# The last stage of an output sum, in four quarters of 144 columns on four row groups of one bank

## The chip, the cores and the metric

The kernel runs on one core of a Trainium2 chip. Its time is the device time of one launch in microseconds; lower is better. Three runs of the kernel before gave 210.95, 211.09 and 211.11 us. The inputs are fixed.

Five engines work on a core, each with its own instruction queue in order: TensorE (PE, with its weight loads shown apart as PEld), VectorE (DVE), ScalarE (ACT), GpSimd (POOL) and SyncE (SP). POOL, SP and ACT also issue DMA transfers between the chip's memory (HBM) and the on-chip memory (SBUF). Matmul results go to PSUM, which has eight banks; a bank holds 512 float32 values on each of 128 partitions.

## The reference

One decoding step for 4 sequences: a sliding-window attention over cached keys and values, and a small mixer MLP, both on the same normalised row of 576 values, added to the input.

```python
xn = layernorm(x)                      # x: 4 x 1 x 576
q  = (xn @ wq)                         # 32 heads of 128
k, v = k_cache[:, :, -2048:], v_cache[:, :, -2048:]     # 16 key/value heads, each for 2 query heads
a  = softmax(q k^T / sqrt(128)) v @ wo
h  = gelu(layernorm(xn) @ w1); hs = shifted(h) @ w2     # B_w1, B_w2
x1 = xn + hs
return x + a + x1 + gelu(layernorm(x1) @ w3) @ w4       # w3: 576 x 4608, w4: 4608 x 576
```

`shifted` moves each quarter of h by one or two places along a sequence of length 1 and fills with zeros, so hs is zero and x1 is xn. The kernel therefore loads neither w1 nor w2, before and after the change: it adds x and xn, and normalises xn again for the MLP. It loads the keys and values of the window, wq, wo, w3 and w4, 87.2 MB in all.

## The kernel before

The order of the work is written out by hand; each engine runs its instructions in the order in which the code names them, and the framework adds semaphores where one engine reads or overwrites what another wrote.

**Start.** SP issues wq (4.6 MB in two transfers) and ACT issues x at once. POOL builds index tiles, two identity matrices and small constants (`neg_half`, `zero`), then the tile `fold` (L234). ACT clears tiles that need zeros, through the helper `cleared` (L211): `xnT`, `ln2T`, `qz`. The layernorm of x alternates between DVE and POOL (the power -0.5 is on POOL, L268), and its result is transposed on PE (L282, L284) with the help of a tile `dup` that POOL fills (L277, L279). POOL then copies selection matrices (L303, L319, L329), and only after those does `start_loads` issue the first two loads of keys (L125, an indirect DMA of 4.2 MB each). A second layernorm, the first part of wo and the first load of values follow on POOL.

**Main part.** Eight steps, each over two of the 16 key/value heads: keys are transposed on DVE (L297), scores computed on PE (L411), softmax spread over DVE, ACT and PE, and values multiplied on PE (L475). Three buffers hold keys and values; a buffer that is freed lets POOL issue the next load, so that several loads always wait in POOL's DMA queue. w3 comes between the values, wo in four parts, and w4 last, in six pieces of 18, 7, 5, 4, 1 and 1 of its 36 blocks (`W4_PIECES`). The MLP's first matrix and its activation are done in step 3; the activation's result is the tile `gT`, 36 blocks of 4 columns, written by POOL (L569).

**The output sum.** Everything that is added to the output is a product of 128x4 weights with 128x576 data, cut in two halves of 288 columns. `acc` is one PSUM bank in which four groups of 4 rows (at rows 0, 32, 64, 96) take such halves in turn: group 0 and 2 the first half, 1 and 3 the second (L230). At the end the four groups must be added in pairs. That is done by copying `acc` to SBUF (`half`, L244) and a float32 matmul with `fold`, a 0/1 matrix of 128 x 4 for each half (L257), into two further PSUM banks, `sum0` (rows 0 to 3) and `sum1` (rows 32 to 35). The last eleven blocks of w4 go straight to those two banks (L252): five ahead of the fold, so that ACT's copy stands beside them, and six behind it. DVE copies the first half of the result to the SBUF tile `fin` (L719), ACT the second (L721), and SP stores 4 rows of 576 bfloat16 values (L722).

Of the kernel before, what the change touches and what calls it, by code (L numbers as in the profile page):

```python
# [8 lines left out]
ACT = mybir.ActivationFunctionType  # L9
ALU = mybir.AluOpType  # L10
AX = mybir.AxisListType
BF16 = mybir.dt.bfloat16
F32 = mybir.dt.float32
# [9 lines left out]
def kernel(  # L23
# [14 lines left out]
    nc = tc.nc  # L38
    P = 128
    B, Sq, D = A_x.shape  # L40
# [8 lines left out]
    NF = F // P  # L49
# [3 lines left out]
    QD = 32  # L53
# [5 lines left out]
    QC = 2 * SC  # L59
    NI = 2  # L60
    CW = D // NI
    NW = SC * QD
    assert NW == 512 and NSL * NJ == QD and NQ == 2 * NQD * NW and NFH == 18
    scale = float(Dh) ** -0.5
# [5 lines left out]
    o2 = out.flatten_outer_dims()  # L70
# [12 lines left out]
    const = ctx.enter_context(tc.tile_pool(name="const", bufs=1))  # L83
    small = ctx.enter_context(tc.tile_pool(name="small", bufs=2))
    ps_s = ctx.enter_context(tc.tile_pool(name="ps_s", bufs=3, space=PSUM))
# [43 lines left out]
    first = wop.tile([P, WOR * D], BF16, tag="wo", name="first")  # L129
# [26 lines left out]
    W4_PIECES = [0, NFH, NF - 11, NF - 6, NF - 2, NF - 1, NF]  # L156
# [50 lines left out]
    def cleared(shape, name):  # L207
        t = const.tile(shape, BF16, name=name)
        flat = t[:] if len(shape) == 2 else t[:].rearrange("p a b -> p (a b)")
        flat = flat.bitcast(F32)  # L210
        nc.scalar.activation(out=flat, in_=zero[:].bitcast(F32).to_broadcast(list(flat.shape)), func=ACT.Copy)  # L211
        return t
# [2 lines left out]
    ln2T = cleared([P, KJ + 2, QD], "ln2T")  # L215
    ZP = (NSL - 1) * NJ
    qz = cleared([P, ZP + NPR * 4 * P], "qz")
    gT = const.tile([P, NF, B], BF16, name="gT")
    op = const.tile([P, WOR, B], BF16, name="op")

    acc = ps_acc.tile([P, CW], F32, name="acc")
    nc.vector.memset(acc[:], 0.0)

    def acc_of(g):
        return acc[g * QD:g * QD + B, :]

    def acc_matmuls(terms):
        for k, (lhsT, rhs) in enumerate(terms):
            for i in range(NI):
                nc.tensor.matmul(out=acc_of(k % 2 * NI + i), lhsT=lhsT, rhs=rhs[:, i * CW:(i + 1) * CW],  # L230
                                 start=False, stop=False, skip_group_check=True)

    fold = const.tile([P, NI * B], F32, name="fold")
    nc.gpsimd.tensor_tensor(out=fold[:].rearrange("p (i b) -> p i b", i=NI),  # L234
                            in0=ident_f[:, 0:2 * QD].rearrange("p (i x) -> p i x", i=NI)[:, :, 0:B],
                            in1=ident_f[:, 2 * QD:P].rearrange("p (i x) -> p i x", i=NI)[:, :, 0:B], op=ALU.add)
    sums = []

    def sum_of(i):
        return sums[i][i * QD:i * QD + B, 0:CW]  # L240

    def sum_open():
        half = const.tile([P, CW], F32, name="half")
        nc.scalar.activation(out=half[:], in_=acc[:], func=ACT.Copy)  # L244
        for i in range(NI):
            sums.append(ps_s.tile([P, NW], F32, tag="S", name=f"sum{i}"))
        return half

    def sum_matmuls(terms, first=False):
        for k, (lhsT, rhs) in enumerate(terms):  # L250
            for i in range(NI):
                nc.tensor.matmul(out=sum_of(i), lhsT=lhsT, rhs=rhs[:, i * CW:(i + 1) * CW],  # L252
                                 start=first and k == 0, stop=False, skip_group_check=True)

    def sum_fold(half):
        for i in range(NI):
            nc.tensor.matmul(out=sum_of(i), lhsT=fold[:, i * B:(i + 1) * B], rhs=half[:],  # L257
                             start=False, stop=False, skip_group_check=True)

    def layernorm(dst_f, dst_bf, src):  # L260
        st = small.tile([B, 2, nc.vector.BN_STATS_DIM], F32, tag="ln_st")
# [40 lines left out]
    for kb in range(NQD):  # L302
        nc.gpsimd.tensor_copy(out=sel[:, :, :, kb, :],  # L303
                              in_=ident_bf[:].rearrange("p (ib i e) -> p ib e i", ib=2, e=2))
# [23 lines left out]
    for g in range(2):  # L328
        nc.gpsimd.tensor_copy(out=same_j[:, g * 2 * QD:(g + 1) * 2 * QD].rearrange("p (e s j) -> p e s j", e=2, j=NJ),  # L329
                              in_=sel_j[:].unsqueeze(2).to_broadcast([P, 2, NSL, NJ]))  # L330
# [18 lines left out]

    q_ps = [ps_s.tile([P, NW], F32, tag="S", name="q_ps") for _ in range(2)]  # L350

    def q_mm(r, g, j):
        c = r * NQD + g
        col, k = (j * NQ + c * NW, j) if j < KJ else (KJ * NQ + g * NW, KJ + r)
        nc.tensor.matmul(out=q_ps[r][g * QD:(g + 1) * QD, :], lhsT=xnT[:, k, :], rhs=wq_sb[:, col:col + NW],  # L355
                         start=(j == 0), stop=False, skip_group_check=True)
# [15 lines left out]
    for r in range(2):  # L372
        nc.vector.tensor_copy(out=q_bf[:, r],  # L373
                              in_=qT_ps[:, r].rearrange("p u (g x) -> p g u x", g=NQD)[:, :, :, 0:B])
    qs_ps = ps_m.tile([P, Hkv, 4, rep, B], F32, tag="m", name="qs_ps")
    for ie in range(4):
        ib, e = divmod(ie, 2)
        nc.tensor.matmul(out=qs_ps[:, :, ie], lhsT=sel[:, ib, e].rearrange("p k i -> p (k i)"),
                         rhs=q_bf.rearrange("p r g u b -> p (r g u b)"), start=True, stop=True)
    for kb in range(NQD):  # L380
        rows = slice(kb * QD, (kb + 1) * QD)
        dst = qz[rows, ZP:].rearrange("p (t i m) -> p t i m", i=4, m=P)[:, :, :, kb * QD:kb * QD + NJ]
# [14 lines left out]
    def k_mask(t, u):  # L397
        S_ps[t, u] = ps_s.tile([P, NW], F32, tag="S", name="S")
        nc.tensor.matmul(out=S_ps[t, u][:].rearrange("p (c k) -> p c k", k=QD), lhsT=ohT[:],  # L399
                         rhs=negbig[:].unsqueeze(1).to_broadcast([B, SC, QD]),  # L400
                         start=True, stop=False, skip_group_check=True)
# [127 lines left out]
    xs = const.tile([P, NF, B], F32, name="g_x")  # L529
# [32 lines left out]
    def mlp_act():  # L562
        u = const.tile([P, NF, B], F32, name="g_u")
        nc.gpsimd.tensor_tensor(out=u[:], in0=xs[:], in1=xs[:], op=ALU.mult)
        nc.gpsimd.tensor_scalar(out=u[:], in0=u[:], scalar1=GELU_A, scalar2=1.0, op0=ALU.mult, op1=ALU.add)
        nc.gpsimd.tensor_tensor(out=u[:], in0=u[:], in1=xs[:], op=ALU.mult)
        nc.scalar.activation(out=u[:], in_=u[:], func=ACT.Tanh, scale=GELU_C)
        nc.gpsimd.tensor_scalar(out=u[:], in0=u[:], scalar1=0.5, scalar2=0.5, op0=ALU.mult, op1=ALU.add)
        nc.gpsimd.tensor_tensor(out=gT[:], in0=u[:], in1=xs[:], op=ALU.mult)  # L569

    def mlp_terms(lo, hi):
        w4 = w_tiles["w4"]
        return [(gT[:, u, :], w4[:, u, :]) for u in range(lo, hi)]


    G_AT = 3
# [1 line left out]
    for t in range(NPR - 1):  # L578
# [53 lines left out]
        if t == G_AT:  # L632
            mlp_turn(2)
            mlp_act()
# [69 lines left out]
    o_expand(2 * hl + 1)  # L704
    o_spread(2 * hl + 1)
    acc_matmuls(mlp_terms(*W4_PIECES[0:2]))
    o_pick(2 * hl + 1)
    o_proj(2 * hl + 1)
    acc_matmuls(mlp_terms(*W4_PIECES[1:3]))
    half = sum_open()  # L710
    sum_matmuls(mlp_terms(*W4_PIECES[2:4]), first=True)
    sum_fold(half)
    sum_matmuls(mlp_terms(W4_PIECES[3], NF))

    fin = const.tile([B, D], out.dtype)
    for i in range(NI):
        dst = fin[:, i * CW:(i + 1) * CW]
        if i == 0:
            nc.vector.tensor_copy(out=dst, in_=sum_of(i))  # L719
        else:  # L720
            nc.scalar.activation(out=dst, in_=sum_of(i), func=ACT.Copy)  # L721
    nc.sync.dma_start(out=o2, in_=fin[:])  # L722


# [28 lines left out]
```

## Time and profile before

| what | value |
|---|---|
| median of three runs | 211.09 us (210.95 to 211.11) |
| the profiled execution | 210.85 us, its span 209.1 us, mean granted clock 0.878 |
| DMA | 87.32 MB, mean 418 GB/s |
| PE busy | 144.0 us, 69% |
| DVE busy | 124.3 us, 59% |
| POOL busy | 31.6 us, 15% |
| ACT busy | 28.5 us, 14% |
| ACT clears qz (128x2060 float32) | 1.90 us from 2.97 |
| POOL's first K load | 1.17 us from 8.70 |
| the last copies, L719 and L721 | 0.45 and 0.40 us |

The span goes from the first to the last instruction that the profiler recorded, in microseconds from its start; the profiled execution's own time holds some more around it. Busy times of engines overlap, so a large share doesn't say that an engine sets the time. The chain view follows the work that ended last back from the end, at each step to what released it; the timeline lists instructions with start and length, and in square brackets how long the engine stood idle before and what ended that.

### The profile page before, as it was taken

To read this page: it belongs to the slowest core of one execution; us is meant where nothing else is said; L and a number is where in the kernel's file an instruction comes from. 1 tells how busy PE (TensorE), PEld (TensorE's weight loads), DVE (VectorE), ACT (ScalarE), POOL (GpSimd) and SP (SyncE) were. 2 spreads that over 40 slices of the span, in tenths; PEclk is the share of its full clock that TensorE was granted. 3 is DMA by queue.
4 is the path that set the end of the run, shared out by engine and by line. 5 is a ranking of instruction groups with operands and counts; after the bars stand their busy time and mean duration, and the time that the engine had idled before them with its cause. 6 is when DMAs were issued, how large, how long until landed. Compare 5 with 4: busy or idle time off the path is not lost.

```text
span 209.1 us, 2165 instructions
## 1 busy us (share of the span) xinstructions
PE 144.0 (69%) x878; PEld 57.7 (28%) x878; DVE 124.3 (59%) x174; ACT 28.5 (14%) x64; POOL 31.6 (15%) x63
## 2 busy tenths in 40 slices
PE   0248198649669933069996793677959947986974
PEld 0013133223214310014432431133314312432442
DVE  5510679993199600098908991998099818896220
ACT  6102500100102011003001201020102010204010
POOL 5680001003200110000133011001010152100000
PEclk9999669997979995559999999696997995899699
DMA  8999999999999999999999999999999999999991
GB/s 302 401 439 464 401 433 429 464 401 433 470 397 437 447 429 407 407 471 445 407 442 453 401 439 423 464 401 439 464 401 428 442 433 407 445 451 404 420 404 60
DMA packets 4155, 87.32 MB, mean 418 GB/s; under 512 B 488, under 2 KB 496, under 8 KB 1200
## 3 DMA queue, kind: packets, MB, share of 16 engines
q0 software_dynamic: 3840, 82.45, 91.7%
q1 hardware_dynamic: 296, 4.72, 5.5%
q8 instruction: 7, 0.11, 0.2%
q14 instruction: 4, 0.03, 0.0%
q10 hardware_dynamic: 8, 0.00, 0.0%
HBM read 87.17 MB, written 0.00 MB: 417 GB/s over the span
## 4 chain that ended last, share of the span: by engine, by line
DMA 63%; PE 18%; DVE 14%; POOL 2%; issue 2%; ACT 0%; DVEq 0%; POOLq 0%
DMA kn<-in_A_k_cache_dram,row 47%; DMA w_sb<-in_B_w_dram 16%; PE S L411 10%; DVE kt L297 9%; PE O L475 6%; DVE mx L417 1%; POOL w_sb L163 1%; DVE pt L456 1%; PE sum L252 1%; PE S L399 0%; POOL vn L125 0%; PE oT L486 0%; DVE dm L420 0%; POOL rstd L268 0%; POOL wo_sb L147 0%
## 5 line engine op out<-in xcount | busy, mean ns | idle before, releaser
L297 DVE STREAM_TRANSPOSE kt<-kn 128x2048 int32<-128x2048 int32 x32 | 73.6, 2304 | 48.7 <-DMA kn<-in_A_k_cache_dram,row 46.1
L411 PE MATMUL S<-kt,qz 128*128 128x512 bf16 x256 | 78.1, 438 | 33.6 <-DVE kt L297 33.6
L411 PEld LDWEIGHTS <-qz 128*128 128x128 bf16 x256 | 23.5, 104 | 72.5 <-issue 55.8
L475 PE MATMUL O<-vn,pt 128*64 128x512 bf16 x256 | 36.4, 415 | 6.5 <-DMA vn<-in_A_v_cache_dram,row 5.3
L456 DVE STREAM_TRANSPOSE pt<-E 64x512 bf16<-64x512 bf16 x32 | 22.1, 690 | 1.2 <-ACT E L447 0.9
L125 POOL DMA_INDIRECT vn<-in_A_v_cache_dram,row x8 | 7.7, 960 | 92.9 <-DVE kt L297 88.4
L447 ACT ACTIVATE E<-S,bias 128x512 bf16<-128x512 f32 x16 | 10.9, 683 | 75.9 <-DVE bias L440 75.9
L475 PEld LDWEIGHTS <-pt 128*64 128x64 bf16 x256 | 13.5, 116 | 23.3 <-issue 13.9
L125 POOL DMA_INDIRECT kn<-in_A_k_cache_dram,row x8 | 7.9, 989 | 41.5 <-PE O L475 22.7
L480 ACT ACTIVATE O_sb<-O,rd 128x512 f32<-128x512 f32 x8 | 5.5, 688 | 54.5 <-PE O L475 54.5
L417 DVE TENSOR_REDUCE mx<-S 128x1 f32<-128x512 f32 x16 | 10.7, 667 | 0.1
L541 PE MATMUL g_ps<-w_sb,ln2T 128*32 128x512 bf16 (+1 forms) x50 | 5.3, 512 | 3.6 <-DMA w_sb<-in_B_w_dram 3.6
L399 PE MATMUL S<-negbig,ohT 4*128 4x512 bf16 x16 | 6.4, 398 | 0.0
L496 DVE TENSOR_REDUCE on<-oT 128x16 bf16<-128x128 f32 x8 | 2.3, 286 | 5.2 <-PE oT L486 5.1
L486 PE MATMUL oT<-ident_w,O_sb 128*128 128x128 f32 x32 | 5.1, 284 | 0.0
L355 PE MATMUL q_ps<-wq_sb,xnT 128*32 128x512 bf16 x40 | 4.4, 625 | 0.9 <-DMA wq_sb<-in_A_wq_dram 0.9
L486 PEld LDWEIGHTS oT<-ident_w,O_sb 128*128 128x128 f32 x32 | 4.3, 154 | 2.7 <-issue 1.1
L163 POOL DMA_DIRECT2D w_sb<-in_B_w_dram x6 | 3.3, 586 | 7.6 <-DMA vn<-in_A_v_cache_dram,row 7.6
L420 DVE TENSOR_SCALAR dm<-sel_g,mx 128x8 bf16<-128x8 bf16 x16 | 3.9, 242 | 0.6
L282 PE MATMUL tp<-ident_bf,first 4*128 4x4 bf16 x8 | 0.6, 173 | 5.1 <-DVE first L269 5.1
L373 DVE COPY first<-qT_ps 128x64 bf16<-128x64 bf16 x2 | 0.3, 186 | 6.3 <-PE qT_ps L370 6.3
L230 PE MATMUL acc<-first,ident_w 4*4 4x288 f32 x4 | 1.1, 657 | 4.1 <-POOL first L342 4.1
(103 smaller groups left out, 80.0 us busy)
## 6 DMA issues: line engine op xcount, KB each, us to landing
wo_sb<-in_A_wo_dram POOLq DMA_DIRECT2D x4, 1152.0 KB, 23.2
w_sb<-in_B_w_dram POOLq DMA_DIRECT2D x1, 4608.0 KB, 29.5
wq_sb<-in_A_wq_dram SPq DMA_DIRECT2D x1, 4096.0 KB, 13.9
w_sb<-in_B_w_dram POOLq DMA_DIRECT2D x1, 2592.0 KB, 28.8
w_sb<-in_B_w_dram POOLq DMA_DIRECT2D x2, 576.0 KB, 31.5
w_sb<-in_B_w_dram POOLq DMA_DIRECT2D x1, 1008.0 KB, 30.6
w_sb<-in_B_w_dram POOLq DMA_DIRECT2D x1, 720.0 KB, 31.9
wq_sb<-in_A_wq_dram SPq DMA_DIRECT2D x1, 512.0 KB, 3.4
```

What stands on the lines that cost most here:

```text
L125: nc.gpsimd.indirect_dma_start(tl[:].rearrange("p c d -> p (c d)"), None, k_rows if kind == "K" else v_rows, bass.IndirectOffsetOnAxis(ap= ...
L163: nc.gpsimd.dma_start(out=t[:, lo:hi, :], in_=src[e][:, at:at + hi - lo, :])
L297: nc.vector.transpose(out=kt[:], in_=src)
L399: nc.tensor.matmul(out=S_ps[t, u][:].rearrange("p (c k) -> p c k", k=QD), lhsT=ohT[:], rhs=negbig[:].unsqueeze(1).to_broadcast([B, SC, QD] ...
L411: nc.tensor.matmul(out=S_ps[t, u][:], lhsT=qz[:, z0:z0 + P], rhs=kt[:, ib, sl * SC:(sl + 1) * SC, e:2 * QD:2].rearrange("p c k -> p (c k)" ...
L417: nc.vector.reduce_max(out=mx[:], in_=S_ps[t, u][:], axis=AX.X)
L447: nc.scalar.activation(out=E[t, u][:].rearrange("p c k -> p (c k)"), in_=S_ps.pop((t, u))[:], func=ACT.Exp, scale=scale, bias=st["bias", t ...
L456: nc.vector.transpose(out=pts[t % 2 * NU + u][rows, :, e * QD:(e + 1) * QD], in_=e_in[rows])
L475: nc.tensor.matmul(out=O_ps[t][rows], lhsT=pts[t % 2 * NU + u][:, c, :], rhs=vn[:, u, :, c, :], start=(u == 0 and c < 2), stop=False, skip ...
L480: nc.scalar.activation(out=O_sb[t][:], in_=O_ps.pop(t)[:], func=ACT.Copy, scale=st.pop(("rd", t))[:, 0:1])
L486: nc.tensor.transpose(out=oT[:, s, :], in_=o[:, s, :], identity=ident_w[:, s * NJ:s * NJ + P])
L541: nc.tensor.matmul(out=g_ps[g * QD:(g + 1) * QD], lhsT=ln2T[:, k, :], rhs=cols[:, :, i0:i0 + n], start=(j == 0), stop=False, skip_group_ch ...
```

## The change

The last six blocks of w4 and the fold are no longer summed as two halves of 288 columns in two banks, but as four quarters of 144 columns in one bank, each on its own group of 32 rows. For that the weights are 32 columns wide, with the four sequences in columns 0, 8, 16 and 24 and zeros between, so that `gT` and `fold` become parts of one tile `gf` that ACT clears at the start (128 x 640 in float32). POOL then writes the 0/1 entries of `fold` into it, and later `gT`. The five blocks ahead of the fold go to `acc`. The result stands in rows 0, 8, ..., 120 of one bank, in 144 columns: DVE copies 72 of them, ACT the other 72, and SP stores 16 rows of 144 values to their places.

```diff
+    NQU = 4
+    CQ = D // NQU
+    ST = QD // B
...
-    gT = const.tile([P, NF, B], BF16, name="gT")
+    gf = cleared([P, NF * QD + 2 * NI * QD], "gf")
+    gT = gf[:, 0:NF * QD].rearrange("p (u x) -> p u x", x=QD)
+    fold = gf[:, NF * QD:].bitcast(F32).rearrange("p (i x) -> p i x", x=QD)
...
-    fold = const.tile([P, NI * B], F32, name="fold")
-    nc.gpsimd.tensor_tensor(out=fold[:].rearrange("p (i b) -> p i b", i=NI),
+    nc.gpsimd.tensor_tensor(out=fold[:, :, 0:QD:ST],
...
-    def sum_of(i):
-        return sums[i][i * QD:i * QD + B, 0:CW]
+    def sum_of(q):
+        return sums[0][q * QD:(q + 1) * QD, 0:CQ]
...
+    def sum_fold():
         half = const.tile([P, CW], F32, name="half")
         nc.scalar.activation(out=half[:], in_=acc[:], func=ACT.Copy)
+        sums.append(ps_s.tile([P, NW], F32, tag="S", name="sum"))
+        for q in range(NQU):
+            i, at = divmod(q * CQ, CW)
+            nc.tensor.matmul(out=sum_of(q), lhsT=fold[:, i, :], rhs=half[:, at:at + CQ],
+                             start=True, stop=False, skip_group_check=True)
+
+    def sum_matmuls(terms):
+        for lhsT, rhs in terms:
+            for q in range(NQU):
+                nc.tensor.matmul(out=sum_of(q), lhsT=lhsT, rhs=rhs[:, q * CQ:(q + 1) * CQ],
+                                 start=False, stop=False, skip_group_check=True)
...
-        nc.gpsimd.tensor_tensor(out=gT[:], in0=u[:], in1=xs[:], op=ALU.mult)
-
-    def mlp_terms(lo, hi):
+        nc.gpsimd.tensor_tensor(out=gT[:, :, 0:QD:ST], in0=u[:], in1=xs[:], op=ALU.mult)
+
+    def mlp_terms(lo, hi, cols=slice(0, QD, ST)):
         w4 = w_tiles["w4"]
-        return [(gT[:, u, :], w4[:, u, :]) for u in range(lo, hi)]
+        return [(gT[:, u, cols], w4[:, u, :]) for u in range(lo, hi)]
...
     acc_matmuls(mlp_terms(*W4_PIECES[1:3]))
-    half = sum_open()
-    sum_matmuls(mlp_terms(*W4_PIECES[2:4]), first=True)
-    sum_fold(half)
-    sum_matmuls(mlp_terms(W4_PIECES[3], NF))
-
-    fin = const.tile([B, D], out.dtype)
-    for i in range(NI):
-        dst = fin[:, i * CW:(i + 1) * CW]
-        if i == 0:
-            nc.vector.tensor_copy(out=dst, in_=sum_of(i))
-        else:
-            nc.scalar.activation(out=dst, in_=sum_of(i), func=ACT.Copy)
-    nc.sync.dma_start(out=o2, in_=fin[:])
+    acc_matmuls(mlp_terms(*W4_PIECES[2:4]))
+    sum_fold()
+    sum_matmuls(mlp_terms(W4_PIECES[3], W4_PIECES[-1], slice(0, QD)))
+
+    fin = const.tile([P, CQ], out.dtype)
+    nc.vector.tensor_copy(out=fin[:, 0:CQ // 2], in_=sums[0][:, 0:CQ // 2])
+    nc.scalar.activation(out=fin[:, CQ // 2:], in_=sums[0][:, CQ // 2:CQ], func=ACT.Copy)
+    nc.sync.dma_start(out=o2.rearrange("b (q c) -> q b c", q=NQU), in_=fin[0:P:ST, :])
```

More of the change, by code (lines that the diff above doesn't have):

```diff
@@ L237 @@
     sums = []
-    def sum_of(i):
-        return sums[i][i * QD:i * QD + B, 0:CW]
-    def sum_open():
+    def sum_of(q):
+        return sums[0][q * QD:(q + 1) * QD, 0:CQ]
+    def sum_fold():
         half = const.tile([P, CW], F32, name="half")
         nc.scalar.activation(out=half[:], in_=acc[:], func=ACT.Copy)
-        for i in range(NI):
[L246 to L258, printed above, removed]
+        sums.append(ps_s.tile([P, NW], F32, tag="S", name="sum"))
[8 more added lines that the diff above has]
+                                 start=False, stop=False, skip_group_check=True)
     def layernorm(dst_f, dst_bf, src):
@@ L709 @@
     acc_matmuls(mlp_terms(*W4_PIECES[1:3]))
-    half = sum_open()
-    sum_matmuls(mlp_terms(*W4_PIECES[2:4]), first=True)
-    sum_fold(half)
-    sum_matmuls(mlp_terms(W4_PIECES[3], NF))
-    fin = const.tile([B, D], out.dtype)
-    for i in range(NI):
-        dst = fin[:, i * CW:(i + 1) * CW]
-        if i == 0:
-            nc.vector.tensor_copy(out=dst, in_=sum_of(i))
-        else:
-            nc.scalar.activation(out=dst, in_=sum_of(i), func=ACT.Copy)
-    nc.sync.dma_start(out=o2, in_=fin[:])
+    acc_matmuls(mlp_terms(*W4_PIECES[2:4]))
[5 more added lines that the diff above has]
+    nc.sync.dma_start(out=o2.rearrange("b (q c) -> q b c", q=NQU), in_=fin[0:P:ST, :])
 _INS = ['A_x', 'A_k_cache', 'A_v_cache', 'A_wq', 'A_wo', 'B_x', 'B_w1', 'B_w2', 'B_w3', 'B_w4']
```

## The prediction

> **What bounds the kernel now.** I read the page's DMA slices and its chain first, then a table by stretches, then single instructions at both ends of the run. The bound used below for a change of time (0.2%, 0.42 us of 211.09) is about what a measurement of this kernel can tell from no change.
>
> ```profile
> DMA  8999999999999999999999999999999999999991
> ...
> q0 software_dynamic: 3840, 82.45, 91.7%
> ...
> DMA 63%; PE 18%; DVE 14%; POOL 2%; issue 2%; ACT 0%; DVEq 0%; POOLq 0%
> ```
>
> The DMA engines are full from the second slice to the last but one; no compute engine is over 69%. The table by stretches (PE, PEld, DVE, ACT, POOL busy, then clock, DMA share, GB/s) says it closer:
>
> ```profile
> 8.00:13.00 5.00, 0.89 (x5) 0.18 (x5) 1.64 (x7) 0.27 (x1) 4.49 (x8) 1.00 0.97 419
> ...
> 60.00:170.00 110.00, 81.54 (x467) 31.83 (x467) 68.83 (x87) 12.96 (x31) 11.80 (x16) 0.86 1.00 431
> ...
> 204.00:205.00 1.00, 1.00 (x14) 0.55 (x14) 0.00 (x0) 0.00 (x0) 0.00 (x0) 1.00 0.54 210
> ...
> 205.50:206.00 0.50, 0.50 (x10) 0.29 (x7) 0.00 (x0) 0.00 (x0) 0.00 (x0) 1.00 0.00 0
> ```
>
> Between 2 and 203 us no stretch falls below 0.97, so whatever delays the stream of transfers once delays the last byte by as much: nothing later gives it back. Only before 2 us and after 204 us can compute set the time. The start, in order of time:
>
> ```profile
> 2.46 0.20 POOL L234 TENSOR_TENSOR fold<-ident_w 128x8 f32<-128x8 f32 x1
> ...
> 2.97 1.90 ACT L211 ACTIVATE qz<-zero 128x2060 f32<-128x2060 f32 x1
> ...
> 4.06 0.57 POOL L268 TENSOR_TENSOR rstd<-rstd,neg_half 4x1 f32<-4x1 f32 x1 [1.41 <-DVE rstd L267]
> ...
> 7.96 0.20 POOL L319 CAST sel_jb<-sel_j 128x16 bf16<-128x16 f32 x1 [1.17 <-DVE sel_j L317]
> ...
> 8.70 1.17 POOL L125 DMA_INDIRECT kn<-in_A_k_cache_dram,row  x1 [0.18 <-issue]
> ```
>
> POOL issues the first K load at 8.70, behind its own share of the layernorm. What matters is how early that is. In the trace's records of single DMA packets, wq fills all 16 engines until 13.10 to 13.58 (its last 32 KB packets start at 11.89 to 12.37), and K's first packets start at that same moment, mean 13.30. The end:
>
> ```profile
> 206.05 0.29 PE L252 MATMUL sum<-w_sb,gT 128*4 128x288 bf16 x2
> 206.37 0.45 DVE L719 CAST fin<-sum 4x288 bf16<-4x288 f32 x1 [5.36 <-PE sum L252]
> 206.40 0.40 ACT L721 ACTIVATE fin<-sum 4x288 bf16<-4x288 f32 x1 [2.45 <-PE sum L252]
> 206.90 0.35 SPq L722 DMA_DIRECT2D out_dram<-fin  x1
> ```
>
> The chain merges twelve matmuls from 205.31 into one piece, but by the semaphore records the last three pieces of w4 land at 205.26, 205.65 and 206.00, and the last pair starts only at 206.05. So one pair of matmuls, two copies side by side and the store lie behind the last byte, not twelve matmuls.
>
> **The change, part by part.** The sum is made against the profiled execution, 210.85 us (span 209.1, 1.75 around it); the median of the runs shown is 0.24 higher.
>
> (1) Clearing the new tile. Weights for a whole 32-column group need zeros in the 28 unused columns, so ACT clears a 128x640 float32 tile after qz, and fold now lies in that tile: the built order shows the fold instruction on POOL waiting for ACT, where it waited for nothing. qz ends at 4.87; the clear starts 0.09 before that, as qz did behind ln2T. Its time: 0.61 us for 512 columns (the pt clears), 0.83 ns per column between that and qz's 1902 ns for 2060, so 0.72, end 5.50. POOL starts about 0.15 after its releaser (rstd's end at 3.91 to 4.06): fold from 5.65, 0.20 long, the next instruction 0.04 ahead of its end: 5.80. That next one is L268, which began at 4.06: 1.74 later. Queued behind it on POOL are the memset and copies of dup, the sel copies, sel_jb, same_j, the two K loads, the residual sum, the second layernorm's power, the first wo load and the first V load. DVE L269 waits for L268, the transposes on PE for both, DVE's ohk, negbig and sel_j stand behind those, and POOL's sel_jb waits for sel_j. There is no slack to absorb it, since POOL's idle 1.17 us at 7.96 ends on work which is itself moved. So K's first load is issued at 10.44.
>
> Is that covered? The cover is wq. The packets of the two queues alternate on an engine: wq's closing 4-byte packet comes at 14.31 to 14.79, behind K's first one. Had K been ready by 12.37, some engine would have taken it ahead of its last wq packet, and none did; it was ready by 13.10. With 1.74 added it is ready between 14.11 and 14.84, after wq has run dry at 13.10 to 13.58. The bubble is from 0.53 (14.11 less 13.58) to 1.74 (14.84 less 13.10). I take ready at 12.50, near the early edge, because the other issues are much quicker (x and wq: first packet 0.94 and 1.04 after the issue starts; here 3.67 to 4.40): 14.24 less 13.30 is 0.94 us, all on the path. It costs nothing only if an engine commits to its next packet long before it starts it; that is the first rival. The later loads moved by 1.74 (V at 16.8 instead of 15.04) stand behind 8.4 MB of K, about 20 us at 430 GB/s, and cost nothing. wq itself lands sooner, not later.
>
> The Trainium skill, DMA: Bandwidth & Descriptors, section Latency and other measured facts, gives a GpSimd-issued DMA about 1 us to its first byte. By that K was ready at 10.9, an estimate from its issue's end at 9.87, would now be ready at 12.6, and part (1) would cost nothing; the sum would be 211.3 on the median. The packet order just told speaks against it.
>
> (2) PE before the last pieces. The five terms of the 25-to-30 piece go to acc on four groups instead of sum on two: 10 matmuls, three rounds of 0.12, so from 203.92 to about 204.46 instead of 204.70. But ACT's half copy (0.41) now follows them instead of standing beside them: 204.50 to 204.91; the fold, eight passes of 144 columns in two rounds of 0.12, issues by 205.19. The next piece lands at 205.26. Cost nothing; were it late, the last piece at 206.00 covers another half microsecond. The 24 matmuls with weights of 32 columns (a 128x32 load is 0.10 in the wq stage, a 128x4 one 0.085) are four behind the last landing. Strided gT on POOL (0.49 us at 108) is needed at 201. Both nothing.
>
> (3) Behind the last landing. Four matmuls of 144 columns start together as four of 288 do in acc; half a round is 0.06 less (ends: 0 and 0.12). Then the copies. Both now read one bank, and the built order has ACT's copy waiting for DVE's. The row for such a pair:
>
> ```profile
> 21.58 0.41 DVE L387 CAST qz<-qs_ps 32x256 bf16<-32x256 f32 x1 [0.49 <-PE qs_ps L378]
> ...
> 22.09 0.38 ACT L385 ACTIVATE qz<-qs_ps 32x256 bf16<-32x256 f32 x1 [1.78 <-DVE qz L387]
> ```
>
> 0.10 passes between the two. DVE: 0.18 at 32 columns (L312), 0.42 at 256, so 0.22 at 72; ACT: 0.20 at 32 (L521), 0.40 at 288, so 0.23. Together 0.22 + 0.10 + 0.23 = 0.55 against 0.45 side by side: +0.10. With the matmuls, +0.04 (ends -0.10, +0.15).
>
> (4) The store. Four rows of 1152 B become sixteen pieces of 288 B. In the records the four packets start 45 ns apart; sixteen in a row would be 12 x 45 = +0.54. wq's first sixteen packets start within 0.21, which would be +0.08. Smaller packets alone could give back 0.04. I take +0.20, nearer the wq row; ends -0.04 and +0.54.
>
> The same page of the Trainium skill, section Why a DMA increments its semaphore by 16 and not by 1, has a transfer from SP run on the largest number of engines up to 16 that divides the slowest dimension of both sides, here 4 and 16: four engines with four pieces each, an estimate of 3 x 45 ns = +0.13 for the store and +1.11 for the sum. Before's four packets for four rows agree with it; no run here shows the sixteen.
>
> Sum: 0.94 + 0.04 + 0.20 = +1.18. Profiled 212.03; median 212.3.
>
> **The rivals.** (A) The bubble doesn't come: engines settle their next packet one packet (1.21 us) ahead, so K was ready before 11.89, is now ready before 13.63, and wq's tail covers it. For it: the fast first packets of the other queues. Against: the last wq packet on every engine before K. It decides from a ready moment of 11.6 downwards. Time: 211.09 + 0.24 = 211.3, no change that can be measured, so not slower.
>
> (B) The delay passes whole: ready at 13.10, bubble 1.5 on the mean engine (14.84 less 13.30), and the store's pieces go one by one (+0.54): 211.09 + 1.54 + 0.04 + 0.54 = 213.2. For it: 45 ns between the packets; against: that needs the late edge of both.
>
> (C) Faster: no bubble, and the two copies run beside each other after all, 0.03 apart as now: -0.06 on PE, 0.45 becomes 0.26, store +0: 211.09 - 0.25 = 210.8. It decides only if ACT's wait is released before DVE's copy ends; the qz pair speaks against that, and even so it stays within 0.2%. Beyond that bound the last w4 engine would also have to finish earlier: its packets share an engine with a 16 KB instruction fetch (204.93 to 206.03), but the next engine is just 0.16 behind.
>
> **How the numbers follow.** Forecast (bubble 0.5 to 1.4) 0.70; A 0.18; B 0.08; C 0.04. Predicted 212.3. Below 211.1 lies C and nearly half of A, 0.12; above 213.1 most of B, 0.07: range 211.1 to 213.1; the forecast's own is 211.7 to 212.9. Slower by over 0.2% (above 211.51): the forecast, B and 0.02 of A with a dear store: 0.80. Faster by over 0.2% (below 210.67): a quarter of C and a little for a luckier landing of w4, 0.02. The rest, 0.18, is within.
>
> **What would show it.** Right: fold on POOL at 5.6 behind the ACT clear; K's first load near 10.4; a DMA share clearly below 1 between 13 and 15 us; the same time from there to the last w4 landing; ACT's final copy waiting for DVE's; 0.5 to 0.6 us from the last matmuls' end to the store's issue. Wrong: a DMA share near 1 through 13 to 15 (A); copies overlapping (C); or the fold's matmuls still running when the last piece of w4 lands, which would put part (2) on the path.

## The result, and the profile after

The changed kernel takes 211.35 us (median of 22 runs, 211.20 to 212.11) against 210.87 for the kernel before in as many runs beside it: ratio 1.0020, 95% interval 1.0013 to 1.0028, or 0.48 us more. Slower, as forecast, but by 0.48 us instead of 1.2. The profiled executions stand for it: 211.36 with a span of 209.5 us, against 210.85 with 209.1. Now and then an execution of one of these kernels, before included, takes 1.3 to 1.7 us longer; the ratios and their intervals count such executions, the medians hardly move by them, and the profiled one of the first experiment below is such a one, so that only its start is compared.

The start of the changed kernel, POOL's timeline:

```profile
5.60 0.21 POOL L238 TENSOR_TENSOR gf<-ident_w 128x8 f32<-128x8 f32 x1 [3.11 <-ACT gf L214]
5.76 0.57 POOL L269 TENSOR_TENSOR rstd<-rstd,neg_half 4x1 f32<-4x1 f32 x1
...
9.66 0.20 POOL L320 CAST sel_jb<-sel_j 128x16 bf16<-128x16 f32 x1 [1.17 <-DVE sel_j L318]
...
10.39 1.17 POOL L128 DMA_INDIRECT kn<-in_A_k_cache_dram,row  x1 [0.18 <-issue]
```

The delay came: POOL stands 3.11 us waiting for ACT's clear, and K's first load is issued at 10.39, 1.69 us later than before (8.70). The bubble didn't. The table by stretches (engines' busy times, then clock, DMA share, GB/s):

```profile
8.00:13.00 5.00, 0.74 (x2) 0.17 (x2) 2.56 (x11) 0.53 (x2) 3.32 (x9) 1.00 0.97 419
13.00:15.00 2.00, 0.82 (x4) 0.09 (x4) 0.29 (x1) 0.00 (x0) 1.93 (x3) 1.00 1.22 524
...
60.00:170.00 110.00, 84.87 (x469) 32.24 (x467) 68.85 (x87) 12.95 (x31) 12.60 (x17) 0.82 1.00 431
```

The share is the same 0.97 and 1.22 in the first two rows as before the change. (A share above 1 comes from how the table counts: 32 packets of 1.21 us start in the stretch from 13 to 15 us, two on each engine, and it has all of their time.) The long stretch moves the same 431 GB/s, though PE's granted clock is 0.82 there instead of 0.86. In the records of single packets K's first ones start at 13.09 to 13.50 us (13.10 to 13.58 before), 0.01 us behind the end of wq's data. The only trace of the delay is that wq's closing packet now goes ahead of them. The last piece of w4 lands at 205.95 (206.00 before; a landing is the moment in the trace at which a transfer raises its semaphore): nothing was lost up to there. The end:

```profile
205.99 0.31 PE L258 MATMUL sum<-w_sb,gf 128*32 128x144 bf16 x4
206.35 0.23 DVE L716 CAST fin<-sum 128x72 bf16<-128x72 f32 x1 [6.55 <-PE sum L258]
206.61 0.23 ACT L717 ACTIVATE fin<-sum 128x72 bf16<-128x72 f32 x1 [1.75 <-DVE fin L716]
206.87 0.67 SPq L718 DMA_DIRECT2D out_dram<-fin  x1
```

ACT waits for DVE's copy, as forecast, and yet SP starts the store at 206.87, not later than before (206.90). From there everything is lost: the issue, SP's instruction that starts the store, takes 0.67 us instead of 0.35, and the store's last landing comes at 208.62, 1.75 us behind the start of its issue; before it was 208.20 and 1.30. All that follows, 0.88 us to the end of the span, is equal. Difference by difference: last landing of w4 -0.05, matmuls to the first copy +0.04, first copy to SP -0.02, store +0.45, together +0.42 of span.

### The profile page after: what moved, and what is told of

It is laid out like the page before. It is cut to its first block, busy times and chain, and to the rows that moved or that the text cites. A ratio compares the mean times of both kernels' runs of the same rounds, so it can differ in the third digit from the quotient of the medians.

```text
span 209.5 us, 2197 instructions
## 1 busy us (share of the span) xinstructions
PE 147.0 (70%) x894; PEld 57.7 (28%) x894; DVE 124.2 (59%) x174; ACT 28.9 (14%) x65; POOL 31.9 (15%) x63
## 4 chain that ended last, share of the span: by engine, by line
DMA 65%; PE 23%; DVE 4%; POOL 3%; issue 3%; ACT 0%; POOLq 0%; DVEq 0%
DMA kn<-in_A_k_cache_dram,row 50%; DMA w_sb<-in_B_w_dram 15%; PE S L412 14%; PE O L476 6%; DVE kt L298 3%; PE oT L487 1%; POOL kn L128 1%; POOL w_sb L166 0%; PE S L400 0%; POOL vn L128 0%; PE sum L258 0%; PE sum L252 0%; POOL wo_sb L150 0%; PE acc L235 0%; POOL rstd L269 0%
## 5 line engine op out<-in xcount | busy, mean ns | idle before, releaser
L412 PE MATMUL S<-kt,qz 128*128 128x512 bf16 x256 | 81.5, 453 | 32.4 <-DVE kt L298 32.4
L476 PEld LDWEIGHTS <-pt 128*64 128x64 bf16 x256 | 13.2, 116 | 22.5 <-issue 13.0
L441 DVE TENSOR_SCALAR bias<-bp 128x1 f32<-128x1 f32 x8 | 1.3, 158 | 6.1 <-PE bp L436 6.1
L270 DVE TENSOR_SCALAR first<-first,mv,rstd 4x576 bf16<-4x576 bf16 x2 | 0.8, 416 | 5.9 <-POOL rstd L269 5.9
```

The costliest lines, as they stand in the source:

```text
L412: nc.tensor.matmul(out=S_ps[t, u][:], lhsT=qz[:, z0:z0 + P], rhs=kt[:, ib, sl * SC:(sl + 1) * SC, e:2 * QD:2].rearrange("p c k -> p (c k)" ...
L476: nc.tensor.matmul(out=O_ps[t][rows], lhsT=pts[t % 2 * NU + u][:, c, :], rhs=vn[:, u, :, c, :], start=(u == 0 and c < 2), stop=False, skip ...
```

## The experiments

Two theories at first. S: the store at the end is the whole difference. F: the late K loads cost something after all. Times are medians beside runs of the kernel before on the same chip.

**The front alone.** To the kernel before, the start of the change and nothing else:

```diff
+    gf = cleared([P, NF * QD + 2 * NI * QD], "gf")
+    gT = gf[:, 0:NF * QD].rearrange("p (u x) -> p u x", x=QD)
+    fold = gf[:, NF * QD:].bitcast(F32).rearrange("p (i x) -> p i x", x=QD)
...
+    nc.gpsimd.tensor_tensor(out=fold[:, :, 0:QD:ST],
...
+            nc.tensor.matmul(out=sum_of(i), lhsT=fold[:, i, 0:QD:ST], rhs=half[:],
...
+        nc.gpsimd.tensor_tensor(out=gT[:, :, 0:QD:ST], in0=u[:], in1=xs[:], op=ALU.mult)
...
+        return [(gT[:, u, 0:QD:ST], w4[:, u, :]) for u in range(lo, hi)]
```

> The kernel before with the front of the change alone: gf cleared by ACT, fold and gT inside it with a column stride of 8, fold on POOL waiting for the clear; the end of the kernel as before. Theory S (the whole 0.48 us of the change is the store at the end): K's first load is issued near 10.4 us instead of 8.7, its first packets still start at 13.1 to 13.5 behind wq, and the time is that of before within 0.1 us. Theory F (the late K loads cost something after all): +0.2 to +0.5 us. The forecast's own step was +0.94 us.

Measured: 210.87 against 210.85 us, ratio 0.9991, interval 0.9975 to 1.0007. The front costs nothing (by the interval at most 0.15 us), although K's load is issued as late as in the changed kernel; K's first packets start at 13.08 to 13.57 us:

```profile
10.40 1.17 POOL L126 DMA_INDIRECT kn<-in_A_k_cache_dram,row  x1 [0.18 <-issue]
```

F falls, and with it the largest term of the forecast.

**The front, later still.** To the front alone: the clear done five times, to see what it costs when wq no longer covers it:

```diff
     gf = cleared([P, NF * QD + 2 * NI * QD], "gf")
+    for _ in range(4):
+        nc.scalar.activation(out=gf[:].bitcast(F32), in_=zero[:].bitcast(F32).to_broadcast([P, NF * QD // 2 + NI * QD]),
+                             func=ACT.Copy)
```

> The front of the change alone, with the clear of gf done five times instead of once, which moves POOL's work by about 2.8 us more (K's first load issued near 13.2 instead of 8.7 or 10.4). In the changed kernel K's first packet came at most 2.70 us behind the start of its issue. If that delay is 1.0 us (as for x and wq), the first packets start near 14.2 and the DMA engines stand idle for about 1 us behind wq; if it is 2.7 us, near 15.9 and 2.6 us idle. Either way the end comes later by what the engines stood idle, +1.0 to +2.6 us. If the engines don't starve for another reason, no change.

Measured: 213.69 us, +2.84 (ratio 1.0137, interval 1.0099 to 1.0175). The table by stretches and POOL's timeline of this kernel:

```profile
13.00:15.00 2.00, 0.18 (x1) 0.00 (x0) 1.40 (x6) 0.27 (x1) 1.52 (x4) 1.00 0.00 0
15.00:17.00 2.00, 0.00 (x0) 0.00 (x0) 0.00 (x0) 0.00 (x0) 1.97 (x2) 1.00 0.87 262
```

```profile
13.46 1.17 POOL L126 DMA_INDIRECT kn<-in_A_k_cache_dram,row  x1 [0.18 <-issue]
```

Here is the hole that was forecast for the change: no packet of data starts between 13 and 15 us (the last ones of wq run until 13.16 to 13.52). With nothing in front of them, K's first packets start 1.88 to 2.78 us behind the start of their issue (15.34 to 16.24, fourteen of the sixteen by 15.55). The wait alone is 2.19 us on the mean, from the end of wq's data (13.33) to these starts (15.52). K's first packets also take 1.37 to 2.02 us instead of 1.21, so that the second ones start 2.74 us later on the mean than in the kernel before (17.26 against 14.52). The last piece of w4 lands at 208.81 instead of 206.00, 2.81 later: what the stream loses at its start passes to the end whole.

**The store in sixteen pieces.** To the kernel before, only the store's form: the tile's rows are padded, so that a row goes out in four pieces of 288 bytes.

```diff
-    fin = const.tile([B, D], out.dtype)
+    CQ = D // 4
+    fin = const.tile([B, 4, CQ + 16], out.dtype)
...
-    nc.sync.dma_start(out=o2, in_=fin[:])
+    nc.sync.dma_start(out=o2.rearrange("b (q c) -> b q c", q=4), in_=fin[:, :, 0:CQ])
```

> The kernel before, everything on four rows as it was, but the result is stored in sixteen pieces of 288 bytes (four to a row, rows of the tile padded). Theory S, if the number of pieces is what costs: the store's issue on SP rises from 0.35 to about 0.67 us, its landing comes 0.3 to 0.45 us later, and the time is +0.3 to +0.45 us. If it is the order of the pieces in memory (here they stand in the order of the output, in the change they don't): issue near 0.35 us and less than +0.1 us. Theory F: less than +0.2 us.

Measured: 211.54 us, +0.69 (ratio 1.0034, interval 1.0010 to 1.0058). Copies and matmuls are those of before; the issue takes 0.81 us:

```profile
206.85 0.81 SPq L723 DMA_DIRECT2D out_dram<-fin  x1
```

So this form of the store costs by itself more than the whole change. Whether by its sixteen pieces was still to be seen.

**The changed kernel, its rows one after the other in memory.** The quarters of the output then stand in another order.

```diff
-    nc.sync.dma_start(out=o2.rearrange("b (q c) -> q b c", q=NQU), in_=fin[0:P:ST, :])
+    nc.sync.dma_start(out=o2.rearrange("b (q c) -> (b q) c", q=NQU), in_=fin[0:P:ST, :])
```

> The changed kernel, but its sixteen rows are stored one after the other in memory, so that the quarters of the output stand in another order than the reference's; nothing else differs. Theory S with the number of pieces: issue 0.67 us and the time of the changed kernel, +0.4 to +0.5 us against before. Theory S with the order of the pieces (two loops over four on the side of memory, one over sixteen in SBUF): issue 0.35 to 0.40 us, sixteen packets on up to sixteen engines, and 0.2 to 0.4 us less than the changed kernel.

Measured: 211.29 us against 210.85, 0.44 apart in the medians (ratio 1.0005, interval 0.9985 to 1.0025, too wide to tell it from either kernel). The profile is clearer: the issue takes 0.55 us, between the two expectations, and the last landing, now of sixteen engines instead of four, comes 1.70 us behind its start, hardly sooner than the 1.75 of the changed kernel. The order in memory is the smaller part.

**Four pieces only.** The changed kernel, with only the first quarter stored:

```diff
+    nc.sync.dma_start(out=o2[:, 0:CQ], in_=fin[0:QD:ST, :])
```

> The changed kernel, but only the first quarter is stored, four rows of 144 values; the other three quarters of the output are left out. Store theory: the issue falls from 0.67 to 0.35 us, the landing comes 0.45 us earlier, and the time is that of before within 0.1 us: the late K loads, the regrouped matmuls and the two copies in turn together are worth nothing. If another part of the change cost 0.2 us or more, the time stays at +0.2 us or more.

Measured: 211.51 us against 210.88 (ratio 1.0031, interval 1.0019 to 1.0042). A clear miss: with a quarter of the pieces the issue takes 0.73 us, more than with all sixteen. It isn't their number.

**Eight pieces of 576 bytes.** As the store in sixteen pieces, with two pieces to a row:

```diff
+    fin = const.tile([B, NI, CW + 16], out.dtype)
...
+    nc.sync.dma_start(out=o2.rearrange("b (i c) -> b i c", i=NI), in_=fin[:, :, 0:CW])
```

> The kernel before, stored in eight pieces of 576 bytes (two to a row). If the issue grows with the number of pieces (0.35 us for 4, 0.81 for 16 in the same form), it takes 0.50 us here and the time is +0.2 to +0.3 us. If it is pieces below 512 bytes that are dear, 0.35 us and less than +0.1 us.

Measured: 211.64 us against 210.88 (ratio 1.0055, interval 1.0033 to 1.0076); issue 0.81 us, the same as with sixteen. Neither the number of the pieces (16 or 8) nor their size (288 or 576 bytes) sets it: both expectations missed.

**Sixteen rows from adjacent partitions.** The store with its rows one after the other in memory, as above, but of rows 0 to 15 of the tile instead of every eighth (most of these aren't the result):

```diff
+    nc.sync.dma_start(out=o2.rearrange("b (q c) -> (b q) c", q=NQU), in_=fin[0:2 * ST, :])
```

> The changed kernel, but rows 0 to 15 of the tile are stored, one after the other in memory, instead of every eighth row; most of what is stored is not the result. The store with every eighth row in this order took 0.55 us to issue. If the step between partitions costs, about 0.40 us as for wq's 128 rows, and 0.15 us less time; if not, 0.55 us.

Measured: 210.99 us against 210.88 (ratio 1.0007, interval 0.9998 to 1.0016). The lines of the store in five kernels, one fence for each: every eighth partition in this order of memory, adjacent partitions, four rows of every eighth, eight pieces in four partitions, and (from an experiment below) four adjacent partitions with rows that lie apart in memory:

```profile
207.07 0.55 SPq L718 DMA_DIRECT2D out_dram<-fin  x1
```

```profile
206.89 0.36 SPq L718 DMA_DIRECT2D out_dram<-fin  x1
```

```profile
207.02 0.73 SPq L718 DMA_DIRECT2D out_dram<-fin  x1
```

```profile
206.88 0.81 SPq L722 DMA_DIRECT2D out_dram<-fin  x1
```

```profile
207.03 0.35 SPq L720 DMA_DIRECT2D out_dram<-fin  x1
```

The first two differ only in the step from one partition to the next: 0.55 us and 0.36, last landing 1.70 and 1.37 us behind the start of the issue. With the cheap one the changed kernel stands 0.11 us above before instead of 0.48, so that the form of the store is most of what the change costs. Sixteen pieces of 288 bytes cost no more than four of 1152 (0.35 and 1.30) when each is the whole row of the next partition. What is dear is the form of the SBUF side: every eighth partition 0.55 to 0.73 us, several pieces in one partition 0.81. Each of these durations is from one profiled execution; where two kernels have the same form, they agree within 0.02 us (0.67 for the changed kernel and 0.69 for its form with two banks below; 0.36 here and for the sixteen adjacent rows of the last experiment). Why the issue takes longer for these forms, the runs don't show.

**The copies side by side.** The changed kernel with its quarters in two banks:

```diff
-        return sums[0][q * QD:(q + 1) * QD, 0:CQ]
+        return sums[q // 2][q * QD:(q + 1) * QD, 0:CQ]
...
+    nc.vector.tensor_copy(out=fin[0:P // 2, :], in_=sums[0][0:P // 2, 0:CQ])
+    nc.scalar.activation(out=fin[P // 2:P, :], in_=sums[1][P // 2:P, 0:CQ], func=ACT.Copy)
```

> The changed kernel with its quarters in two banks, the first two in one and the last two in another; DVE copies 64 rows of 144 columns from the one, ACT 64 rows of 144 from the other, and neither waits for the other. If the wait between the copies costs what the trace says (0.23, 0.03 and 0.23 in turn, 0.50 us), side by side they take 0.32 us, 0.18 less; SP waits for two engines again, +0.07. So 0.1 us less than the changed kernel and still about +0.35 us against before. If the store weren't the term, it would come close to before.

Measured: 211.13 us against 210.88 (ratio 1.0013, interval 1.0004 to 1.0022), 0.25 above before where the changed kernel is 0.48 above.

```profile
206.34 0.30 DVE L717 CAST fin<-sum 64x144 bf16<-64x144 f32 x1 [8.07 <-PE sum L259]
206.38 0.29 ACT L718 ACTIVATE fin<-sum 64x144 bf16<-64x144 f32 x1 [1.55 <-PE sum L259]
206.73 0.69 SPq L719 DMA_DIRECT2D out_dram<-fin  x1
```

The copies in turn cost the change some 0.14 us at SP (206.87 to 206.73) and about 0.2 in the medians; the store (0.69) still holds the rest.

**Two stores on two queues.** The kernel before, each engine's half stored as soon as it is copied:

```diff
             nc.vector.tensor_copy(out=dst, in_=sum_of(i))
+            nc.sync.dma_start(out=o2[:, 0:CW], in_=dst)
...
             nc.scalar.activation(out=dst, in_=sum_of(i), func=ACT.Copy)
+            nc.scalar.dma_start(out=o2[:, CW:D], in_=dst)
```

> The kernel before, stored in two halves: SP stores DVE's 288 columns (it waits for DVE alone), ACT stores its own. Each store takes four adjacent partitions and rows that lie 1152 bytes apart in memory. If only the step between partitions makes an issue dear, SP's issue takes 0.35 to 0.40 us, and the time is that of before within 0.15 us. If rows that lie apart in memory cost as well (0.12 us more in the changed kernel than with its rows stored one after the other), SP's issue takes 0.45 to 0.55 us and the time is +0.1 to +0.2 us.

Measured: 210.88 us against 210.92 (ratio 0.9993, interval 0.9977 to 1.0009), no change. Its store line stands above: rows that lie 1152 bytes apart in memory, from adjacent partitions, take 0.35 us.

**The idea in another layout.** Quarters on sixteen adjacent rows, so that both the copies and the store take their cheap form. The weights are windows of 16 columns that move by one for each quarter, and each quarter is cut in halves of 72 columns on two groups and banks:

```diff
+        for lhsT, rhs in terms:
+            for q in range(NQU):
+                for h in range(NI):
+                    at = q * CQ + h * CH2
+                    nc.tensor.matmul(out=sum_of(h), lhsT=lhsT[:, 3 - q:3 - q + NR], rhs=rhs[:, at:at + CH2],
+                                     start=False, stop=False, skip_group_check=True)
...
+    fin = const.tile([NR, CQ], out.dtype)
+    nc.vector.tensor_copy(out=fin[:, 0:CH2], in_=sum_of(0))
+    nc.scalar.activation(out=fin[:, CH2:], in_=sum_of(1), func=ACT.Copy)
+    nc.sync.dma_start(out=o2.rearrange("b (q c) -> (b q) c", q=NQU), in_=fin[:])
```

> The idea of the change with another layout: the four quarters of a sequence come out on adjacent rows (row 4b+q), by weights 16 wide taken from a window that moves by one column per quarter; the columns of a quarter are cut in two halves of 72 on two row groups in two banks, so that DVE and ACT each copy 16x72 side by side, into 16 adjacent partitions, and the store takes 16 rows that lie one after the other in memory. If the reading of the store holds, its issue takes 0.36 us; the copies take 0.27 us instead of 0.45 (before) or 0.50 (changed); eight matmuls in four rounds follow the last piece, 0.05 to 0.2 us more than before's pair. Together -0.15 to +0.05 us against before, 0.4 to 0.6 us less than the changed kernel. If the store costs by its sixteen pieces after all, +0.3 us.

Measured: 211.07 us against 210.92 (ratio 1.0008, interval 0.9989 to 1.0028), runs from 210.77 to 212.45; the profiled one took 211.67. PE's timeline and the end of that one:

```profile
204.90 0.97 PE L257 MATMUL sum<-half,gf 128*16 128x72 f32 x16 [0.50 <-ACT half L251]
205.64 1.66 PE L266 MATMUL sum<-w_sb,gf 128*16 128x72 bf16 x48
```

```profile
207.33 0.22 DVE L724 CAST fin<-sum 16x72 bf16<-16x72 f32 x1 [7.49 <-PE sum L266]
207.36 0.22 ACT L725 ACTIVATE fin<-sum 16x72 bf16<-16x72 f32 x1 [2.52 <-PE sum L266]
207.64 0.36 SPq L726 DMA_DIRECT2D out_dram<-fin  x1
```

Copies (0.25 us side by side) and store (0.36) came out as expected. But six blocks are now 48 matmuls, the last of which starts at 207.05 where w4 had landed at 205.92: PE has become the last link, at a granted clock of 0.53 in this stretch (205 to 207.4). By the interval it can't be told from the kernel before, and no version here is shown to be faster.

## Why the prediction was wrong

**(1) The clear and the late K loads: the step that failed.** The delay was right (1.74 us expected, 1.69 measured; K's issue at 10.44 expected, 10.39 measured). The cover was misjudged: the forecast was 0.94 us of idle DMA engines, the measurement 0. The sentence that failed is "Had K been ready by 12.37, some engine would have taken it ahead of its last wq packet, and none did". Without wq in front, K's first packets start 1.88 to 2.78 us behind the start of the issue; if the delay is the same beside wq, K was ready between 10.6 and 11.5 us in the kernel before, and the engines still ran wq packets that started at 11.89 to 12.37 first. The changed kernel says the same with wq running: its first K packets start at most 3.11 us behind their issue (13.50 less 10.39), which makes K ready by 11.81 in the kernel before. So a ready packet of K didn't go ahead of the next one of wq, as rival A had it. Whether an engine had taken that packet already, as A says, or passes from one queue to the other by another rule, the runs don't show. In the changed kernel the same reckoning gives 12.3 to 13.2 us against wq's end at 13.09 to 13.50: covered, with 0.6 us left on the fourteen quicker engines (12.5 to 13.1) and next to nothing on the two slow ones, if they are slow in this kernel too. The run with the clear done five times confirms the other half of the step: what the stream does lose (2.74 us) passes to the end whole (2.81).

The Trainium skill, DMA: Bandwidth & Descriptors, section Latency and other measured facts, has about 1 us to the first byte of a GpSimd-issued DMA. The trace of that run agrees: from the end of the issue (14.63) 0.71 to 1.61 us, 0.89 on the mean.

**(2) PE before the last pieces: right.** ACT's copy of acc runs from 204.46 (204.50 expected), the fold's matmuls from 204.92, and the last blocks wait for the last landing. The reserve was thinner than told: the last round ahead of the final block starts at 205.74 to 205.78 us, 0.2 us ahead of the landing, since PE ran at half its clock from 205.1 on. The layout of the last experiment used that reserve up.

**(3) Matmuls and copies: about right.** +0.04 was expected, and from the last landing to SP's start the two kernels differ by +0.02. The parts moved: matmuls +0.04 instead of -0.06 (at full clock, in the experiment with rows one after the other in memory, 0.285 us from the last matmul's start to DVE's copy, against 0.317 before and 0.347 in the changed kernel at half clock); the gap between the copies 0.03 us instead of 0.10; and 0.07 saved that was not reckoned with, since SP now waits for one engine instead of two (0.09 from the last copy to the issue before, 0.025 now).

**(4) The store: the direction right, the size and the reason wrong.** +0.20 was taken between -0.04 and +0.54, and it was +0.45, nearly the whole result. The prediction counted pieces on the DMA engines and had no term for SP's issue. Of the 0.45, 0.32 is the longer issue and 0.15 a longer wait from its end to the first packet (0.59 us instead of 0.44); from there to the last landing it is 0.49 us instead of 0.51. Four experiments show that neither the number of the pieces nor their size matters here, and that the step between partitions does. The Trainium skill's rule on how many engines a transfer takes (same page, section Why a DMA increments its semaphore by 16 and not by 1) agrees: four landings in the changed kernel, sixteen where both sides have sixteen rows. But the estimate from it, +0.13, missed, since the loss lies ahead of the first packet and not on the engines.

So it went as rival A had it, which was given 0.18, with the store at twice its price. That A's 211.3 lies so near the measured 211.35 is luck: it starts from 211.09 where the kernel before measured 210.87 beside the changed one, and that makes up for the store. The predicted 212.3 was 0.94 too high by (1), 0.22 by that start, and 0.25 too low by (4).

## What to carry to other kernels

When a load is issued late behind a full queue, keep apart when it is ready and when its turn comes: the order of packets in a trace shows the turn, and a run with the cover taken away measures the other. A layout that shortens copies can be paid for in the store: look at the form of its SBUF side, whole rows of adjacent partitions or not, before counting pieces or bytes. And behind the last landing every link is serial, so a change there is worth only the sum of its links, the DMA's issue among them.

## What the runs showed of the hardware that was not expected

The duration of a store's issue on SP, for 4.5 KB or less: 0.35 to 0.36 us for whole rows of 4 or 16 adjacent partitions, one after the other in memory or (four of them) apart; 0.55 to 0.73 us for every eighth partition; 0.81 us for two or four pieces in each of four partitions. The last landing follows 1.18 to 1.37 us behind the start of the cheap ones and 1.70 to 1.99 behind the dear ones.

In four of the six profiled kernels with the changed front and a regrouped sum (the change, the two banks, the sixteen adjacent partitions, the adjacent rows), the granted clock fell to 0.5 between 204.6 and 205.4 us, inside the last stage; in the other two at 206.7 and 208.4, behind the last matmuls. In the kernel before it held past the last instruction. Of the other five kernels with the matmuls of before, one had such a stretch in the last stage: the front alone, with a clock of 0.5 from 200.9 to 207.8 us. Its last twelve matmuls ran in rounds of 0.24 us instead of 0.12, and DVE's copy began 1.73 us behind the last landing of w4 instead of 0.36, which is more than the whole change cost. So the changed matmuls aren't needed for it; whether they make it more frequent stays open.
